# The turn between two layers: heads added early, a narrower last step, one more chunk kept

## The chip, the cores and the metric

The kernel runs on one core of one Trainium2 chip. The metric is device time in microseconds (us). A core has engines with a queue of instructions each: TensorE (PE; weight loads are shown as PEld), VectorE (DVE), ScalarE (ACT), GpSimd (POOL) and SyncE (SP), which here issues the loads. Loads go through one queue that is spread over 16 DMA engines. On-chip memory has 128 partitions; matrix products land in PSUM banks.

## The reference

Two tokens (B = 2) pass twice through the same pair of layers, in float32: attention over a cache, then a gated feed-forward block, each with a layer norm (no scale) and a residual.

```
B, D, H, Sk, Dh, F = 2, 448, 16, 4096, 256, 1792
attention:  q = (layernorm(x) @ wq) by head;  p = softmax(q . k_cache / 16)
            x = x + concat_over_heads(p @ v_cache) @ wo
block:      g = layernorm(x) @ W_gate;  g = g * (g > 0)
            x = x + (g * (layernorm(x) @ W_up)) @ W_down
order:      attention, block, attention, block (same caches and weights both times)
```

Keys and values of one head and token are 4 MB each. There are 32 such pairs, "units", so each attention reads 256 MB of cache, and the kernel has to read it twice except for what stays on chip.

## The kernel before

**The store.** On-chip memory holds an "arena" of 24 places of 1 MB ("units" in the code: 128 partitions by 2048 floats) and three single places of 896 KB (128 by 1792 floats). Keys and values of a unit come in four chunks of 1 MB (NC = 4), or as 2, 4 or 8 chunks in one load. A load of weights is 896 KB: seven for gate and up ("in"), four for down ("out", the last a half), one for the query and output weights of a head or pair of heads ("h", "q", "o").

**The order of loads.** A list (`pending`) is written by hand: all of the first attention, the first block's eleven weight loads, all of the second attention, the second block. `pump` (L159 issues on SP) walks down the list as long as the next load finds a place. `release` frees a place and calls `pump`, so a load is issued at the point of the program where a place becomes free, and on SP it waits until the engine that last read the place is done. The list is strict: a load that finds no place holds back all behind it.

**What stays on chip.** The second attention takes the units in the order: last four first. So the keys and values that the first attention reads last need not be loaded again. `keep` lists the chunks that stay: 20 chunks and the weights of the last head, and the last chunk (c = 3) of the values of `second[2]`. The other three chunks of those values (`rest`, c = 0, 1, 2) are let go at the turn, their places take 896 KB weight loads, and only the overwritten 896 KB of each is loaded again to the same place (`left_at`). With 21 chunks and a head kept, five places remain through the turn: the three of `rest` and two single ones.

**Attention.** For each unit: products of keys and query (VectorE, with ScalarE's sums), maximum and exponential (POOL, ACT), then `weigh` (L659): for each chunk four matmuls of 512 columns, side by side in four bands of PE's columns, that add p @ v into a bank `po`. For odd units the pair of units of a head is closed: `out_copy` (L673, ACT) copies the first 256 columns of the bank into `row`, `out_add` (L677, DVE) adds the other 256, `out_turn` (L688, PE) turns them into columns, `out_keep` (L701, DVE) divides by the sum of the exponentials, and `project` (L711, PE) multiplies by the output weights into the bank `acc`. `busy(n)` (L361) is a product of n times 64 columns that nobody reads; it only occupies PE.

**The turn.** After the last `project`, `ffn(False)` begins with `absorb` (L369 to L390): ACT copies `acc` to `row` and sums it (L379), PE turns `row` into columns and forms the mean (L381, L369, L371), and DVE adds both to x in its column form `xs` (L389). Then `proj` multiplies x by the gate and up weights (L809), four matmuls for each 896 KB of weights and each of its 128-row parts; the fourth load ("in", 3) holds the last 64 rows of both, and so is used twice, at the end of the gate half and at the start of the up half. Each part's place is released behind its last product. `add_rows` (L394) adds `acc` into the running x in row form (`y`) behind the gate half; `squares` and `deviation` (L405, L406) give the layer norm's scale. Then come the ReLU and product of both halves, the turning of the hidden values (L880), the down products (`block`, L903), and x for the second attention.

**Second attention, first units.** The keys kept are used first; each chunk released lets one of the next loads go, in the order of the program: four chunks of the first unit's keys, then keys of the second unit and values in turn.

Of the kernel before, what the change touches and what calls it, by code (L numbers as in the profile page):

```python
# [10 lines left out]
ALU = mybir.AluOpType  # L11
AX = mybir.AxisListType
# [14 lines left out]
KEPT = 20  # L27
ALONE = 25
SPARED = 12
TINY = 174  # L30
# [50 lines left out]
def two_layers(  # L81
# [55 lines left out]
    def pump(by_half=False):  # L137
        while pending:
            (kind, name, c), n = pending[0]
            last = at_of.get((kind, name, c - 1)) if kind in "kv" else None  # L140
            if kind == "g":
                last = MIDDLE - (name + 1) % 2
            at = units.take(n, kind, last)
            if at is None:
                return
            pending.pop(0)
            src = source((kind, name, c), n)
            assert at == left_at.get((kind, name, c), at)
            start = place(at) + VALUES * DH * (name in spared and n == PAIR)
            dst = arena[:, start : start + src.shape[1]]  # L150
            parts = [0, src.shape[1]]
            if by_half:
                parts[1:1] = [src.shape[1] // 2]
            if not pending:
                parts[1:1] = [src.shape[1] - CLOSE * TAIL]
            elif len(pending) == 1:
                parts[1:1] = [8 * P]
            for i, j in zip(parts, parts[1:]):
                nc.sync.dma_start(dst[:, i:j], src[:, i:j])  # L159
            for k in range(n):  # L160
                key = (kind, name, c + k)
                if n == PAIR:
                    key = ("k", name, k - NC) if k >= NC else ("v", behind[name], k)
                if kind == "g":
                    key = ("q", name, 0) if (name + k) % 2 == 0 else ("o", name - 1, 0)
                at_of[key] = at + k
                if kind == "in" and k:
                    lies_at[key] = start + k * F
            if n >= NC:
                blocks.add((kind, name))  # L170
# [85 lines left out]
    keep.add(("v", second[2], NC - 1))  # L256
    of_second = [(key, n) for key, n in of_second if key not in keep]

    rest = [("v", second[2], c) for c in range(NC - 1)]
    heads = [(key, n) for key, n in of_second if key[0] in "hq"][:2]  # L260
    parts = [(key, 1) for key in rest]
    first_of_second = parts[1:] + heads + parts[:1]
# [148 lines left out]
    def attention(order, after, q_first=None, begun=None):  # L411
# [228 lines left out]
        def weigh(u, c):  # L640


            vt = get("v", order[u], c)
            if (u - n_u, c) in FILL:
                busy(FILL[u - n_u, c])
# [5 lines left out]
            for t in range(CT // 2):  # L651
# [5 lines left out]
                for values, i, j in parts:  # L657
                    if i < j:
# [5 lines left out]
                            stop=(u % 2 == 1 and c == NC - 1),  # L664
                        )
            if ("v", order[u], c) not in after:
                release("v", order[u], c)
            if u >= n_u - 2 and c == NC - 1:
                busy(8)
# [33 lines left out]
        def project(u):  # L703
# [4 lines left out]
            for c in range(2):  # L708
# [4 lines left out]
                    start=(n < 3), stop=(n >= n_u - 3),  # L713
# [3 lines left out]
            if h < GROUPED:  # L717
                if h % 2:
                    release("o", h // 2, 0)
            elif ("h", h, 0) not in after:  # L720
                release("h", h, 0)

# [12 lines left out]
        for u in range(n_u + 2):  # L735

            mixed = ahead and u < HASTE
            if u == n_u - 1 and u not in q_of:
                query(u)
            if_pair(score, u, 0)  # L740
# [48 lines left out]
            if_pair(out_copy, u - 1)  # L789

    def ffn(last):
# [3 lines left out]
        busy(2)  # L795
        total = squares()
        if not last:
# [5 lines left out]
        def proj(p, parts):  # L803

            p = p[:, :D]
            for n, (part, c, done) in enumerate(parts):
                w = get("in", "", part)
# [12 lines left out]
            return p  # L820

# [28 lines left out]
        add_rows(SUMS, lead, stop=last)  # L850
# [164 lines left out]
    attention(first, keep)  # L1015
    attention(second, set(), *ffn(False))
# [67 lines left out]
```

## Time and profile before

| | us |
|---|---|
| median of 3 runs (1313.6 to 1314.62) | 1314.23 |
| profiled execution, its own time | 1314.3 |
| its span (first to last instruction) | 1312.0 |
| DVE busy | 1065.3 (81%) |
| PE busy | 505.6 (39%) |
| POOL busy | 297.9 (23%) |
| ACT busy | 195.2 (15%) |

The bytes read are 560.47 MB, at 427 GB/s over the span. The mean granted clock of TensorE is 0.69 of full speed. The engines' busy times overlap; a busy share says little of what bounds a stretch. The rows further down are copied from the page and from answers of the trace, which can be asked for a window of time, an engine or a line.

### The profile page before, as it was taken

Reading aid. Unit: us, or ns where it says so; the run is one execution under the profiler, and the core shown is the slowest. Engines: PE = TensorE matmul, PEld = TensorE weight load, DVE = VectorE, ACT = ScalarE, POOL = GpSimd, SP = SyncE. Lnnn points to the kernel's source line nnn. Section 1 sums busy time; section 2 is a strip of 40 time slices with the busy share of each in tenths; the row PEclk is TensorE's granted clock in tenths of the full one; section 3 lists DMA queues with packets and bytes.
Section 4 is the critical chain, followed back from the end, with each engine's and each line's share of the span. In section 5 each row is a group of like instructions: output and inputs, shape, how many; then the busy total and the mean of one; then the engine's idle time right before and its main releaser. Section 6 shows DMA issues by size and latency. Waiting matters only on the chain.

```text
span 1312.0 us, 8388 instructions
## 1 busy us (share of the span) xinstructions
PE 505.6 (39%) x3022; PEld 152.0 (12%) x3022; DVE 1065.3 (81%) x711; ACT 195.2 (15%) x789; POOL 297.9 (23%) x169
## 2 busy tenths in 40 slices
PE   3152243332433224324495445322342513433248
PEld 2010010000100001101141101100110100110013
DVE  4988988799897998787619896698999889886892
ACT  1100000010000000122417523000000100012231
POOL 0330412304123040021002151140345304100230
PEclk9665776657766577666697767666676666766669
DMA  9999999999999999999999999999999999999998
GB/s 408 438 432 432 434 426 438 438 426 434 434 430 432 438 432 424 443 420 429 422 399 421 434 427 439 438 436 430 423 443 432 430 430 438 432 432 427 429 421 337
DMA packets 20068, 561.00 MB, mean 428 GB/s; under 512 B 2232, under 2 KB 2364, under 8 KB 6844
## 3 DMA queue, kind: packets, MB, share of 16 engines
q1 hardware_dynamic: 20020, 560.48, 99.5%
q8 instruction: 23, 0.38, 0.1%
q14 instruction: 17, 0.14, 0.0%
q10 hardware_dynamic: 8, 0.00, 0.0%
HBM read 560.47 MB, written 0.00 MB: 427 GB/s over the span
## 4 chain that ended last, share of the span: by engine, by line
DMA 55%; DVE 31%; POOL 7%; PE 4%; issue 2%; ACT 1%; SPq 0%; POOLq 0%; DVEq 0%; ACTq 0%
DMA arena<-in_vk_dram 51%; DVE tiny L538 16%; DVE arena L524 10%; POOL tiny L629 4%; POOL tiny L601 4%; DMA arena<-in_w_in_dram 3%; DVE arena L573 2%; DVE arena L586 2%; DMA arena<-in_w_out_dram 1%; PE small L688 1%; PE po L453 1%; ACT arena L579 1%; DVE row L677 0%; DVE tiny L583 0%; ACT down L617 0%
## 5 line engine op out<-in xcount | busy, mean ns | idle before, releaser
L524 DVE TENSOR_TENSOR arena<-arena 128x8192 f32<-128x8192 f32 (+2 forms) x53 | 450.0, 8492 | 103.4 <-DMA arena<-in_vk_dram 102.6
L538 DVE TENSOR_REDUCE tiny<-arena 128x32 f32<-128x8192 f32 (+1 forms) x54 | 436.5, 8084 | 0.0
L659 PE MATMUL po<-arena,down 128*4 128x512 f32 x2052 | 313.2, 729 | 192.9 <-ACT down L617 116.5
L601 POOL PARTITION_ALL_REDUCE tiny<-tiny x63 | 121.0, 1920 | 719.2 <-DVE tiny L595 718.4
L688 PE MATMUL small<-tiny,row 128*128 128x2 f32 x128 | 30.9, 345 | 558.7 <-DVE row L677 558.7
L629 POOL PARTITION_ALL_REDUCE tiny<-tiny x63 | 149.0, 2364 | 60.4 <-ACT down L617 60.4
L613 ACT ACTIVATE tiny<-tiny 128x1 f32<-128x1 f32 x63 | 18.6, 295 | 734.6 <-POOL tiny L601 734.6
L659 PEld LDWEIGHTS po<-arena,down 128*4 128x4 f32 x2052 | 65.7, 97 | 410.5 <-issue 231.2
L688 PEld LDWEIGHTS small<-tiny,row 128*128 128x128 f32 x128 | 28.1, 306 | 589.1 <-DVE row L677 589.1
L453 PE MATMUL po<-arena,xs 128*33 128x512 f32 (+1 forms) x130 | 65.3, 661 | 0.0
L579 ACT ACTIVATE arena<-arena 128x256 f32<-128x256 f32 x135 | 54.4, 404 | 41.3 <-DVE arena L573 40.4
L711 PE MATMUL acc<-arena,tiny 128*2 128x448 f32 x128 | 51.0, 895 | 21.2 <-DVE tiny L701 21.1
L530 ACT ACTIVATE arena<-arena 128x256 f32<-128x256 f32 x112 | 44.8, 402 | 88.3 <-DVE arena L524 88.3
L465 POOL PARTITION_BROADCAST arena<-arena x32 | 21.8, 749 | 158.5 <-ACT arena L461 147.8
L573 DVE TENSOR_TENSOR arena<-arena 128x1024 f32<-128x1024 f32 (+2 forms) x21 | 32.8, 1560 | 3.4 <-PE acc L711 3.4
L677 DVE SCALAR_TENSOR_TENSOR row<-po,tiny,row 128x256 f32<-128x256 f32 x32 | 15.4, 480 | 22.1 <-ACT row L673 22.0
L461 ACT ACTIVATE arena<-po 33x512 f32<-33x512 f32 x13 | 7.7, 590 | 159.3 <-PE po L453 159.3
L701 DVE TENSOR_TENSOR tiny<-small,tiny 128x4 f32<-128x4 f32 x32 | 5.2, 161 | 28.6 <-PE small L688 28.6
L617 ACT ACTIVATE down<-tiny 128x32 f32<-128x32 f32 x64 | 26.6, 416 | 2.2
L579 ACT ACTIVATION_READ_ACCUMULATOR arena<-arena 128x1 f32 x135 | 25.2, 187 | 0.0
L453 PEld LDWEIGHTS po<-arena,xs 128*33 128x33 f32 x130 | 16.4, 136 | 62.1 <-issue 59.4
L530 ACT ACTIVATION_READ_ACCUMULATOR arena<-arena 128x1 f32 x112 | 21.0, 187 | 0.0
(174 smaller groups left out, 335.8 us busy)
## 6 DMA issues: line engine op xcount, KB each, us to landing
arena<-in_vk_dram SPq DMA_DIRECT2D x17, 4096.0 KB, 38.2
arena<-in_vk_dram SPq DMA_DIRECT2D x16, 2048.0 KB, 32.7
arena<-in_w_pair_dram SPq DMA_DIRECT2D x11, 1792.0 KB, 30.8
arena<-in_vk_dram SPq DMA_DIRECT2D x11, 1024.0 KB, 9.4
arena<-in_w_in_dram SPq DMA_DIRECT2D x12, 896.0 KB, 25.5
arena<-in_vk_dram SPq DMA_DIRECT2D x1, 6528.0 KB
arena<-in_w_head_dram SPq DMA_DIRECT2D x7, 896.0 KB, 22.0
arena<-in_w_out_dram SPq DMA_DIRECT2D x5, 896.0 KB, 19.6
```

The lines of the kernel that those rows point to most:

```text
L453: nc.tensor.matmul(q[:, cols], xs[:, c, :], w_c, start=(i == 0), stop=(i == len(parts) - 1))
L524: nc.vector.tensor_mul(part, part, q_of[u][:, None, :].to_broadcast([P, n, DH]))
L530: nc.scalar.activation(kt[:, t, :], kt[:, t, :], AF.Copy, accum_out=s_of[u][:, t : t + 1])
L538: nc.vector.reduce_sum(found, part, axis=AX.X)
L573: nc.vector.tensor_mul(part[:, :whole, :], kt[:, :whole, :], q_of[u][:, None, :].to_broadcast([P, whole, DH]),)
L579: nc.scalar.activation(part[:, t, :], part[:, t, :], AF.Copy, accum_out=found[:, t : t + 1])
L601: nc.gpsimd.partition_all_reduce(mx_of[u], mx, P, RED.max)
L617: nc.scalar.activation(found, s_of.pop(u).rearrange("p (k r) -> p k r", r=2), AF.Exp, bias=nm, scale=sr[:, b : b + 1], accum_out=rs,)
L629: nc.gpsimd.partition_all_reduce(total[:, b : b + 1], rs, P, RED.add)
L659: nc.tensor.matmul(po_of[u][32 * t : 32 * t + 4, (i - 2 * t) * DH : (j - 2 * t) * DH], p_of[u][:, at : at + 4], values[:, i * DH : j * DH] ...
L688: nc.tensor.matmul(pT_of[u][:, c, :], row[:, c * P : (c + 1) * P], pick[:, b : b + B], start=True, stop=True,)
L711: nc.tensor.matmul(acc[at : at + B], oT_of[h][:, c, :], wo[:, c * D : (c + 1) * D], start=(n < 3), stop=(n >= n_u - 3),)
```

## The change

- `LEFT = 2`: chunks 2 and 3 of the values of `second[2]` stay on chip (22 kept chunks instead of 21), and only chunks 0 and 1 are loaded again. Four places remain through the turn. The order of the first loads of the second layer becomes: weights of a head, two value chunks, weights of a head.
- The last value chunk of the first attention is loaded in two halves. `weigh` works on the first half as before (two matmuls of 512 columns), then the bank is closed and `out_copy` and `out_add` run; the second half goes as four matmuls of 256 columns, one for each 256 values, into another bank.
- `settle=early`: behind the last exponential, before the last unit's values, `early` adds all heads but the last to x (`absorb`, `add_rows`) and computes minus the mean over D of the last head's output weights (`means`).
- `last_out` replaces turning and dividing of the last pair: for each 128 columns a sum on DVE, a turning matmul and a multiplication. There is no `project` of this head into `acc`.
- In `ffn(False)`, `arrive` adds the last head to x part by part, with the output weights as the stationary operand and the head's two columns as the moving one (`give`), and the mean by `means`; part 0 ahead of the first gate product, part 1 and the tails behind it. The running `y` gets the last head by two matmuls behind the gate half, in place of one `add_rows`. `squares` moves behind the gate half.
- The place of head 14's weights is freed without a `pump`; the next `pump` finds it. Fillers of the last two units are cut (8 columns' worth of 64 to 4, two of 8 and one of 5 and 2 go, one of 1 comes).

```diff
+LEFT = 2
-TINY = 174
+TINY = 176
@@ pump
-            if by_half:
+            if by_half or (kind, name, c) == ("v", first[-1], NC - 1):
@@ two_layers
-    keep.add(("v", second[2], NC - 1))
+    keep |= {("v", second[2], c) for c in range(LEFT, NC)}
-    rest = [("v", second[2], c) for c in range(NC - 1)]
+    rest = [("v", second[2], c) for c in range(LEFT)]
-    first_of_second = parts[1:] + heads + parts[:1]
+    first_of_second = heads[:1] + parts + heads[1:]
@@ weigh
+            split = settle and (u, c) == (n_u - 1, NC - 1)
+            closes = bool(settle) and (u, c) == (n_u - 1, NC - 2)
             if (u - n_u, c) in FILL:
-                busy(FILL[u - n_u, c])
+                busy(4 if split else FILL[u - n_u, c])
-            for t in range(CT // 2):
+            for t in range(CT // 4 if split else CT // 2):
...
-                            stop=(u % 2 == 1 and c == NC - 1),
+                            stop=(u % 2 == 1 and c == NC - 1) or (closes and t >= CT // 4),
+            if split:
+                out_copy(u)
+                out_add(u)
+                po_of[u] = po[0]
+                for t in range(CT // 2):
+                    at = 2 * (c * CT + CT // 2 + t) - t % 2
+                    nc.tensor.matmul(
+                        po_of[u][32 * t : 32 * t + 4, :DH],
+                        p_of[u][:, at : at + 4],
+                        vt[:, (CT // 2 + t) * DH : (CT // 2 + t + 1) * DH],
+                        start=True, stop=True,
+                    )
+                return
-            if u >= n_u - 2 and c == NC - 1:
+            if u >= n_u - 2 and c == NC - 1 and not settle:
                 busy(8)
@@ project
+            elif settle and u == n_u - 3:
+                units.free.add(at_of.pop(("h", h, 0)))
+        def last_out():
+            u = n_u - 1
+            h, b = order[u - 1]
+            pT, oT = small(2, B), little("oT", 2, B)
+            for c in range(2):
+                at = slice(c * P, (c + 1) * P)
+                nc.vector.scalar_tensor_tensor(
+                    row[:, at], po_of[u][:, at], fold[:, 0:1], row[:, at],
+                    op0=ALU.mult, op1=ALU.add,
+                )
+                nc.tensor.matmul(pT[:, c, :], row[:, at], pick[:, b : b + B], start=True, stop=True)
+                nc.vector.tensor_mul(oT[:, c, :], pT[:, c, :], r_of[u - 1])
+            busy(1)
+            return oT
@@ attention, loop over u
+            if settle and u == n_u + 1:
+                return last_out()
+            if settle and u == n_u:
+                settle()
+    def early():
+        absorb(acc[:SUMS], SUMS, lead, nlead)
+        add_rows(SUMS, lead)
+        gives = output_weights(H - 1).rearrange("p (c d) -> p c d", c=2)
+        nc.vector.reduce_sum(means, gives, axis=AX.X)
+        nc.vector.tensor_scalar_mul(means, means, -1.0 / D)
@@ ffn
+            wo = output_weights(H - 1)
+            pt = small(DC, B)
+            minus, less = po[0][:, :B], little("less", B)
@@ proj
+                if not last and part < FULL and c == part:
+                    arrive(part)
+        def arrive(part):
+            if part == 0:
+                for c in range(2):
+                    nc.tensor.matmul(
+                        minus, means[:, c : c + 1].to_broadcast([P, P]), oT[:, c, :],
+                        start=(c == 0), stop=(c == 1),
+                    )
+                    give(0, slice(0, P), 0, c)
+                for c in range(2):
+                    give(1, slice(0, P), P, c)
+                nc.vector.tensor_copy(less, minus)
+                add(*spans[0], less[:, None, :].to_broadcast([P, DC, B]))
+                for i in range(2):
+                    add(slice(0, P), slice(i, i + 1), pt)
...
+        def give(i, p, at, c):
+            w = wo[:, c * D + at : c * D + at + p.stop - p.start]
+            nc.tensor.matmul(pt[p, i, :], w, oT[:, c, :], start=(c == 0), stop=(c == 1))
@@ ffn, behind the gate half
-        add_rows(SUMS, lead, stop=last)
+        if last:
+            add_rows(SUMS, lead, stop=True)
+        else:
+            total = squares()
+            for c in range(2):
+                nc.tensor.matmul(y, oT[:, c, :], wo[:, c * D : (c + 1) * D], start=False, stop=False)
@@ end
-    attention(first, keep)
-    attention(second, set(), *ffn(False))
+    means = little("means", 2, bufs=1)
+    oT = attention(first, keep, settle=early)
+    attention(second, set(), *ffn(False, oT))
```

## Rows read from the trace of the kernel before

**Rows 1.** The page: DMA busy share in 40 slices; the queue's packets, MB, share
```profile
DMA  9999999999999999999999999999999999999998
...
q1 hardware_dynamic: 20020, 560.48, 99.5%
```

**Rows 2.** Busy time by window: length, engines' busy us, PEclk, DMA share, GB/s
```profile
672.00:680.00 8.00, 7.19 (x51) 2.81 (x49) 1.50 (x6) 0.69 (x2) 0.00 (x0) 1.00 1.02 423
```

**Rows 3.** The same view by single microseconds (PE, PEld, DVE, ACT, POOL)
```profile
643.00:644.00 1.00, 0.65 (x4) 0.56 (x4) 1.00 (x3) 0.04 (x1) 0.00 (x0) 0.77 1.04 442
...
668.00:669.00 1.00, 0.95 (x10) 0.29 (x12) 0.89 (x6) 0.00 (x0) 0.00 (x0) 1.00 0.73 301
669.00:670.00 1.00, 1.00 (x16) 0.39 (x12) 0.05 (x1) 0.00 (x0) 0.00 (x0) 1.00 0.47 194
670.00:671.00 1.00, 1.00 (x16) 0.19 (x8) 0.00 (x0) 0.00 (x0) 0.00 (x0) 1.00 0.93 208
671.00:672.00 1.00, 1.00 (x10) 0.17 (x2) 0.00 (x0) 0.00 (x0) 0.00 (x0) 1.00 0.81 323
...
677.00:678.00 1.00, 0.57 (x8) 0.16 (x8) 0.00 (x0) 0.00 (x0) 0.00 (x0) 1.00 1.05 437
```

**Rows 4.** The chain that ended last, in order of time: start us, us, what
```profile
661.94 1.09 PE po L659 x8
...
664.10 0.61 PE small L688 x4
...
666.01 0.64 ACT row L379 x2
...
667.08 0.67 PE small L369 x6
...
668.01 0.27 DVE xs L389
...
668.32 1.75 PE po L809 x16
...
680.40 1.09 PE po L903 x28
...
796.93 32.08 DMA arena<-in_vk_dram
```

**Rows 5.** Timelines of ScalarE and of VectorE near 663: start, us, instruction, idle before
```profile
663.05 0.47 ACT L673 ACTIVATE row<-po,tiny 128x256 f32<-128x256 f32 x1 [9.26 <-PE po L659]
...
663.56 0.48 DVE L677 SCALAR_TENSOR_TENSOR row<-po,tiny,row 128x256 f32<-128x256 f32 x1 [9.09 <-ACT row L673]
```

**Rows 6.** Timeline of the load queue SP: start and length of issues
```profile
669.34 1.08 SPq L159 DMA_DIRECT2D arena<-in_w_in_dram  x2
...
673.71 2.63 SPq L159 DMA_DIRECT2D arena<-in_w_out_dram  x3
...
693.60 0.33 SPq L159 DMA_DIRECT2D arena<-in_vk_dram  x1
...
704.36 0.33 SPq L159 DMA_DIRECT2D arena<-in_vk_dram  x1
```

**Rows 7.** Issues at 0.72, 669.34, 670.09, 693.60, 704.36: KB, us to landing
```profile
arena<-in_w_head_dram SPq DMA_DIRECT2D x1, 896.0 KB, 4.8
...
arena<-in_w_in_dram SPq DMA_DIRECT2D x1, 896.0 KB, 5.6
...
arena<-in_w_in_dram SPq DMA_DIRECT2D x1, 896.0 KB, 7.3
...
arena<-in_vk_dram SPq DMA_DIRECT2D x1, 1024.0 KB, 7.4
...
arena<-in_vk_dram SPq DMA_DIRECT2D x1, 1024.0 KB, 7.3
```

**Rows 8.** Timeline of TensorE around the turn
```profile
655.34 1.02 PE L361 MATMUL po<-ident 128*2 128x512 f32 x2
...
671.53 0.92 PE L394 MATMUL acc<-row,tiny 96*2 96x448 f32 x2
```

More of the change, by code (lines that the diff above doesn't have):

```diff
@@ L409, in inverse, with attention @@
         nc.vector.reciprocal(rstd, rstd)
-    def attention(order, after, q_first=None, begun=None):
+    def attention(order, after, q_first=None, begun=None, settle=None):
         nsr = little("nsr", B, bufs=1)
@@ L712, in project @@
                     acc[at : at + B], oT_of[h][:, c, :], wo[:, c * D : (c + 1) * D],
-                    start=(n < 3), stop=(n >= n_u - 3),
+                    start=(n < 3), stop=(n >= n_u - (5 if settle else 3)),
                 )
@@ L788, in attention, with ffn @@
                     if_pair(weigh, u - 1, c)
-            if_pair(out_copy, u - 1)
-    def ffn(last):
+            if not (settle and u == n_u):
+                if_pair(out_copy, u - 1)
+    def early():
         absorb(acc[:SUMS], SUMS, lead, nlead)
-        busy(2)
-        total = squares()
-        if not last:
+        add_rows(SUMS, lead)
+        gives = output_weights(H - 1).rearrange("p (c d) -> p c d", c=2)
+        nc.vector.reduce_sum(means, gives, axis=AX.X)
+        nc.vector.tensor_scalar_mul(means, means, -1.0 / D)
+    def ffn(last, oT=None):
+        if last:
+            absorb(acc[:SUMS], SUMS, lead, nlead)
+            busy(2)
+            total = squares()
[3 more added lines that the diff above has]
+            minus, less = po[0][:, :B], little("less", B)
             h, b = second[0]
@@ L820, in proj, with add @@
             return p
+        def arrive(part):
[12 more added lines that the diff above has]
+                    add(slice(0, P), slice(i, i + 1), pt)
+            elif part == 1:
+                for c in range(2):
+                    give(2, slice(0, P), 2 * P, c)
+                for p, c in spans[1:]:
+                    add(p, c, less[:, None, :].to_broadcast([P, DC, B]))
+                add(slice(0, P), slice(2, FULL), pt)
+            else:
+                for c in range(2):
+                    for p, i in spans[1:]:
+                        give(i.start, p, FULL * P, c)
+                for p, c in spans[1:]:
+                    add(p, c, pt)
+                nc.vector.tensor_copy(xs[:, :, 32:], xs[:, :, 31:32])
+        def give(i, p, at, c):
+            w = wo[:, c * D + at : c * D + at + p.stop - p.start]
+            nc.tensor.matmul(pt[p, i, :], w, oT[:, c, :], start=(c == 0), stop=(c == 1))
+        def add(p, c, part):
+            x_c = xr[p, c]
+            nc.vector.tensor_add(x_c, x_c, part[p, c, :, None].to_broadcast(x_c.shape))
         def between(part):
@@ L849, in ffn @@
         pg = proj(banks[0], [(0, 0, True), (1, 1, True), (2, 2, True), (3, 3, False)])
-        add_rows(SUMS, lead, stop=last)
+        if last:
+            add_rows(SUMS, lead, stop=True)
+        else:
+            total = squares()
+            for c in range(2):
+                nc.tensor.matmul(y, oT[:, c, :], wo[:, c * D : (c + 1) * D], start=False, stop=False)
         if last:
```

## The prediction

> **What bounds the kernel now.** I read the slices of the span first, then the queues, then the chain of waits across the turn between the layers. The DMA digit is 9 in all but the last slice, and one queue holds 99.5% of sixteen engines' span for 560.48 MB [rows 1]: the kernel is a stream of loads, and a change in the time has to be bytes that are not loaded or a stretch in which the stream runs dry. Full, it moves 423 GB/s with the 896 KB loads of the turn [rows 2]. One stretch is not full: from 668 to 672 us the rates are 301, 194, 208 and 323 GB/s [rows 3], 1026 KB where 4 us at 423 would be 1692. So 666 KB, or 1.57 us of a mean engine's time, is lost at the turn.
>
> Why it is dry there: five 896 KB loads of feed-forward weights are issued ahead; the sixth waits until the first gate product has released its place. The chain shows the way to it: the last values' products from 661.94, their copy 663.05, the sum of both halves 663.56, the turning products 664.10, then x is brought up from 666.01, 667.08 and 668.01 to the gate product at 668.32 [rows 4, 5]. The next two loads are issued from 669.34 [rows 6].
>
> Does the loss reach the end? The load issued at 669.34 landed 5.6 us later (674.9); the next, issued 0.75 us behind it, after 7.3 us (677.4) [rows 6, 7]. The first load of the program, onto an empty queue, took 4.8 us; its bytes are 2.17 of that at 423 GB/s, so about 2.6 us is issue and landing. Then 669.34 + 2.6 + 2.17 = 674.1 would have been possible, and 674.9 was measured: for the engine that finishes last the queue was not empty, it had 0.8 us to spare. The dry stretch was idle time of engines that had run ahead. A load has landed when its last engine has, so I count the 1.57 us as mostly no loss, and a small delay there as mostly no cost.
>
> **The change part by part.** *Bytes.* Of the three value chunks that the first layer lets go and the second loads again, one more stays: 917,504 bytes less, 917,504 / 423 GB/s = 2.17 us [rows 2]. The last value chunk comes as two loads with rows half as long; I take a few per cent of its 1 MB (2.48 us at 423 GB/s), 0.1 us, between nothing and the 2.6 us of a load onto an empty queue, and near nothing because the queue is full there. Net -2.1 us. The stream is the bound, so nothing hides this.
>
> By the Trainium skill (DMA: Bandwidth & Descriptors, Anatomy of one DMA) a DMA of the GpSimd path takes about 2.0 us plus its bytes; if that held for each load in this queue, the extra load would cost 2.0 us and the sum would be -0.2. The two loads above landed 2.5 us apart, not 4.2, so here the fixed part lies under the queue.
>
> *One place less.* Four instead of five loads can be issued ahead, so the fifth must be issued 2.17 us earlier than the sixth was, at 667.2, for the queue to stand as before. The shorter turn has to pay for that, and I work out its length.
>
> TensorE before the last values: the last-but-one unit's products end at 655.34, where a 512-column filler starts [rows 8]. Now comes the early sum into x: from the end of the copy (666.01 + 0.64) to 668.0 it takes 1.3 us, and the running sum behind it 0.85 of the 0.92 in its row [rows 4, 8]. Its input, ScalarE's copy of the projections, is ready: that engine is idle for 9.26 us before 663.05 [rows 5]. A 512-column product group occupies 0.86 of the 1.0 in its row, a 256-column one half of that. So: filler 0.43, two value chunks 1.72, filler 0.43, third chunk 0.86, filler 0.43, first half of the last 0.86 (two products side by side last as long as four, since the filler alone shows 1.02). 1.3 + 0.85 + 4.73 = 6.9: 662.2. The half has landed by then. The second half lands where the whole did, about 661.9, and waits 0.3; its narrow products (between 0.5 and 1.0, half the columns with the whole tail) take 0.6, until 662.8.
>
> After that: copy and sum of the first half (0.47 and 0.48, [rows 5]) run beside the narrow products, until 663.3. Then, twice: a 128-column sum (between 0.27 and 0.48, I take 0.35, nearer the row of 96 columns), one turning product (between 0.31 and 0.61, I take 0.38) and a small multiplication (under 0.27, I take 0.2): 0.95 with gaps, 665.2. Then the mean and the first weights as stationary operand, two products at 0.67/3 and a tail, 0.6: 665.8. A copy and two sums into x, 0.6 (0.4 to 0.8, by the 0.27 row): 666.4. From gate product to issue it took 669.34 - 668.32 = 1.02: the issue comes at about 667.45 (666.5 to 668.5), 1.9 us earlier than now and 0.3 later than the 667.2 that would leave all as it is. The last engine has 0.8 us to spare: cost 0, at the late end 0.5. Engines that run ahead idle 0.3 us longer.
>
> *The projection of the last head into y* moves behind the gate products, as two matmuls in place of one: +0.85 us on TensorE. Behind it in line is the first product of the up half, which releases the fourth weights, before at 673.71 [rows 6] and now near 674.55; that now lets the first down weights in. Landings 2.17 us apart put the fourth weights at 674.9 - 4.34 = 670.6 and these at 679.3; 674.55 + 2.6 + 2.17 = 679.3. Nothing is left to spare and nothing is late: 0, up to 0.4. The first load behind the down weights is released by the first down product at 680.40 + 1.09 = 681.5 [rows 4]; due with the stream (679.3 + 2 x 2.17 + 1.1 for the half load + 2.17 = 686.9) it may be issued until 682.1: 0.6 to spare.
>
> *Second layer.* Its start hangs on the last gate/up weights and stays. Its first loads are issued as compute releases places, at the same times as now, while the stream is 2.1 us ahead. Two have the least room [rows 6, 7]: 1 MB issued at 693.60 landed after 7.4 us and one at 704.36 after 7.3; less 2.48 for the bytes and 2.6, that is 2.3 and 2.2 us. Less 2.1, 0.1 to 0.2 remains: cost 0 to 0.5, I take 0.2. Later there is ample room: 8 MB issued at 796.93 took 32 us to land [rows 4], of which 19.8 are bytes.
>
> *Other edits.* The early additions (six of up to 0.27) and the mean over 896 columns (at most 3.5 times the 0.48 of 256) fall on VectorE while it is idle for 9.09 us before 663.56 [rows 5]; without that cover they would cost up to 3.3 us. The fillers that go give nothing back. The order of head and value loads changes; both are wanted after the first units of the second layer.
>
> *Sum.* -2.17 + 0.1 + 0 (turn) + 0 (y) + 0.2 = -1.9 us. The profiled execution took 1314.3 (span 1312.0) against a median of 1314.23, so the two stand alike: 1314.23 - 1.9 = 1312.3.
>
> **Rivals.** *Given back at the next narrow place (17%).* The loads issued at 693.60 and 704.36 come too late for the last engine as well; their times are fixed by compute, so what the turn gains above some 1 us ends there. For it: the spare of 2.2 us equals the gain. Against it: it needs more than the 2.6 us that I take for issue and landing, and that was read off a cold start. Time: -1.0, 1313.2.
>
> *The dry stretch counts and shrinks (17%).* If the engine that ends the kernel is one of those that idled from 668 to 672, and the fifth load is issued before 666.5, some 1.0 of the 1.57 us is gained as well: -3.2, 1311.0. For it: nothing says which engine is last 640 us later. Against it: my sum gives 667.45.
>
> *The stream of four places stalls at half clock (8%): slower.* Place: TensorE between 663 and 675, where fillers go and short products with waits come. The granted clock fell within 643 to 644 us (0.77), with TensorE busy for 0.65 of it; it held 1.00 in 677 to 678 at 0.57 [rows 3]. By the Trainium skill (TensorE: Matmul & The Clock Gate, What's actually happening) the array is throttled unless activity releases it; these two rows alone don't settle it. At 1.2 GHz the work behind the fourth weights (0.85 + 1.7 + 0.85 = 3.4 us) takes 6.8: the first down weights are issued 3.4 us late, the down products and the start of the second layer follow. Price 3.4 to 6: +1.5 to +4, I take +3: 1317.2. It decides once TensorE is at 1.2 GHz for most of 668 to 675; one short drop delays the first issue by 0.9 and is mostly absorbed.
>
> *It brings nothing (6%).* The extra load keeps its fixed cost in the queue, or the four places run dry in turn: -0.2, 1314.0.
>
> **How the numbers follow.** The forecast, -1.5 to -2.5, has 52%. 0.2% is 2.6 us, about what a measurement of this kernel can tell from no change: the forecast and the first and last rivals (75%) lie within it, less 7% for the forecast's upper edge: 68%. Faster than 1311.6: the second rival and that edge, 24%. Slower than 1316.9: 8%. The likeliest case's own range is 1311.7 to 1312.9; to hold 8 in 10 it reaches to 1310.8 (the second rival) and 1314.2 (the give-back and no change).
>
> **What would show it.** Queue bytes 560.48 - 0.92 = 559.56 MB. The fifth gate/up load issued at 667 to 668, the gate product from about 666.4. A dry stretch of about the same depth, some 2 us earlier. The second layer's first loads landing 2 us earlier than now, with less than 0.5 us to spare. Granted clock 1.00 from 654 to 690. The prediction is wrong if the fifth load is issued after 669, if a second dry stretch appears near 675 or 704 to 708, or if the end moves by other than the bytes.

## The result, and the profile after

The changed kernel took 1316.49 us in the median (1314.92 to 1317.98, 14 runs) against 1313.97 for the kernel before (1313.46 to 1314.62, 14 runs): a ratio of 1.0021, interval 1.0014 to 1.0028. It is slower by 2.5 us (1.8 to 3.7), where 1.9 less was forecast. The profiled execution took 1315.26 us, span 1313.5: it is 1.2 us quicker than the median, so its trace can't show all of the loss.

The page has the bytes that were predicted, and the answer to [rows 1] shows nothing else:

```profile
DMA  9999999999999999999999999999999999999998
...
q1 hardware_dynamic: 20020, 559.56, 99.4%
```

0.92 MB less, and the queue is as busy as before. The windows at the turn (columns as in [rows 2, 3]; the last two are DMA busy share and GB/s, the one before them the granted clock) show where the time went:

```profile
667.00:668.00 1.00, 1.00 (x10) 0.36 (x2) 0.10 (x1) 0.00 (x0) 0.00 (x0) 0.82 0.42 172
668.00:669.00 1.00, 1.00 (x8) 0.77 (x11) 0.19 (x1) 0.00 (x0) 0.00 (x0) 0.50 0.82 172
669.00:670.00 1.00, 1.00 (x8) 0.00 (x0) 0.00 (x0) 0.00 (x0) 0.00 (x0) 0.50 0.57 179
...
676.00:677.00 1.00, 1.00 (x13) 0.43 (x17) 0.49 (x3) 0.70 (x2) 0.00 (x0) 1.00 0.57 229
677.00:678.00 1.00, 1.00 (x10) 0.30 (x2) 0.17 (x1) 0.00 (x0) 0.00 (x0) 1.00 0.12 43
678.00:679.00 1.00, 1.00 (x10) 0.16 (x8) 0.00 (x0) 0.00 (x0) 0.00 (x0) 1.00 0.94 165
...
686.00:687.00 1.00, 1.00 (x24) 0.78 (x26) 0.19 (x1) 0.15 (x2) 0.00 (x0) 1.00 1.19 280
```

Three things are to be seen. The stream now runs dry three times, not once. The clock falls from 2.4 to 1.2 GHz at the gate products, within 667 to 668 us. And in 668 to 669 the engines are busy for 0.82 of the time and move 172 GB/s, where 423 GB/s stood beside a share of 1.02 in [rows 2]: a busy DMA engine is not one at its rate.

The chain of waits (start, us, what), against [rows 4]:

```profile
662.04 0.48 ACT row L689
...
666.75 0.96 PE po L864 x8
667.71 0.94 PE small L909 x4
...
670.83 3.14 PE po L864 x16
673.97 1.82 PE acc L948 x4
...
682.82 1.09 PE po L1001 x28
...
690.96 0.42 DVE row L494
```

L864 are the gate and up products (L809 before), L948 the projection into y, L1001 the down products (L903 before), and L494 the copy of the query with which the second layer begins (L493 before). The turn itself is as short as predicted. The down products start 2.42 us later (682.82 against 680.40), although their bytes were to come no later. The load queue (issues: start, length, count) shows the steps between, against [rows 6]:

```profile
667.77 5.10 SPq L160 DMA_DIRECT2D arena<-in_w_in_dram  x3
677.05 4.08 SPq L160 DMA_DIRECT2D arena<-in_w_out_dram  x4
683.92 0.33 SPq L160 DMA_DIRECT2D arena<-in_w_head_dram  x1
...
692.89 15.92 SPq L160 DMA_DIRECT2D arena<-in_vk_dram  x9
```

The load issued at 667.77 landed after (answer to [rows 7])

```profile
arena<-in_w_in_dram SPq DMA_DIRECT2D x1, 896.0 KB, 5.0
```

5.0 us, on the stream's schedule. The two behind it, issued at 670.36 and 672.54, took 4.6 and 6.0 us, so the last of them landed at 678.5. The first down weights were issued at 677.05 where 674.55 was predicted.

What ends this stretch is the second layer's start. VectorE's timeline in the kernel before (start, us):

```profile
688.53 0.42 DVE L493 COPY row<-po 128x256 f32<-128x256 f32 x1 [0.66 <-PE po L959]
688.99 0.42 DVE L586 SCALAR_TENSOR_TENSOR arena<-arena,po 128x256 f32<-128x256 f32 x1
```

From here VectorE works without a gap through the kept units, and each unit it is through with frees the place of the next load: the first such load is issued 1.94 us after the copy in both kernels (690.47 before, 692.89 after, the copy at 688.53 and 690.96). The chain of the kernel before shows why this start can matter, and the prediction did not use it. From the copy on the chain is compute, most of it VectorE's:

```profile
688.99 7.96 DVE arena L586 x46
...
742.59 1.13 DVE arena L573
...
796.50 0.43 ACT arena L461
```

No load stands in it until the one that [rows 4] shows at 796.93. In the change the same chain reaches that load at 798.53, 1.60 us later, from a start 2.43 us later; the span is 1.5 us longer in this execution, and the median 2.5. The runs had to tell whether the start is the cause, and why 2.17 us of bytes show nowhere.

### The profile page after: what moved, and what is told of

Its sections match the earlier page's. It is cut to its first block, busy times and chain, and to the rows that moved or that the text cites. A ratio compares the mean times of both kernels' runs of the same rounds, so it can differ in the third digit from the quotient of the medians.

```text
span 1313.5 us, 8441 instructions
## 1 busy us (share of the span) xinstructions
PE 511.6 (39%) x3042; PEld 156.8 (12%) x3042; DVE 1068.7 (81%) x726; ACT 195.0 (15%) x789; POOL 303.7 (23%) x169
## 3 DMA queue, kind: packets, MB, share of 16 engines
q1 hardware_dynamic: 20020, 559.56, 99.4%
## 4 chain that ended last, share of the span: by engine, by line
DMA 52%; DVE 31%; POOL 7%; PE 7%; issue 2%; ACT 1%; SPq 0%; POOLq 0%; DVEq 0%; ACTq 0%
DMA arena<-in_vk_dram 49%; DVE tiny L539 15%; DVE arena L525 10%; POOL tiny L630 5%; POOL tiny L602 2%; DMA arena<-in_w_in_dram 2%; DVE arena L574 2%; PE po L662 2%; DVE arena L587 2%; DMA arena<-in_w_out_dram 1%; PE small L704 1%; PE po L864 1%; ACT arena L580 1%; DVE row L693 1%; DVE tiny L584 0%
## 5 line engine op out<-in xcount | busy, mean ns | idle before, releaser
L602 POOL PARTITION_ALL_REDUCE tiny<-tiny x63 | 95.0, 1508 | 712.9 <-DVE tiny L596 712.1
L630 POOL PARTITION_ALL_REDUCE tiny<-tiny x63 | 180.6, 2867 | 60.3 <-ACT down L618 60.3
```

The lines of the kernel that those rows point to most:

```text
L602: nc.gpsimd.partition_all_reduce(mx_of[u], mx, P, RED.max)
L630: nc.gpsimd.partition_all_reduce(total[:, b : b + 1], rs, P, RED.add)
```

## The experiments

Fourteen more kernels ran. The kernel before, run beside them, took 1313.79 to 1313.95 in the median. "Start" below is the copy that begins the second layer, read from VectorE's timeline of each profiled execution, and "traced" is the time of that same execution; "places" are loads that can be ahead at the turn.

| run | MB | places | start | traced us | median us | ratio, interval |
|---|---|---|---|---|---|---|
| before | 560.48 | 5 | 688.53 | 1314.3 | 1313.9 | |
| the change | 559.56 | 4 | 690.96 | 1315.26 | 1316.49 | 1.0021 (1.0014 to 1.0028) |
| e10 before, a load left out at the turn | 559.56 | 5 | 688.74 | 1314.03 | 1314.53 | 1.0003 (0.9994 to 1.0012) |
| e14 before, as much left out later | 559.56 | 5 | 688.46 | 1311.69 | 1311.65 | 0.9982 (0.9973 to 0.9991) |
| e16 before, start delayed | 560.48 | 5 | 690.76 | 1316.65 | 1316.65 | 1.0018 (1.0009 to 1.0027) |
| e9 one place more | 561.4 | 6 | 688.25 | 1316.3 | 1315.82 | 1.0016 (1.0007 to 1.0024) |
| e15 e9, start delayed | 561.4 | 6 | 690.04 | 1316.16 | 1316.46 | 1.0019 (1.0010 to 1.0028) |
| e8 before, gate 0.86 later | 560.48 | 5 | 689.14 | 1313.81 | 1313.81 | 1.0000 (0.9991 to 1.0009) |
| e13 before, gate 2.15 later | 560.48 | 5 | 692.18 | 1316.8 | 1314.93 | 1.0010 (1.0001 to 1.0019) |
| e1 change, fillers | 559.56 | 4 | 691.99 | 1316.48 | 1315.51 | 1.0014 (1.0005 to 1.0022) |
| e6 e1, y later | 559.56 | 4 | 690.78 | 1316.56 | 1315.93 | 1.0017 (1.0008 to 1.0027) |
| e2 change, five places | 560.48 | 5 | 690.59 | 1315.12 | 1315.71 | 1.0015 (1.0006 to 1.0024) |
| e7 e2, fillers | 560.48 | 5 | 690.80 | 1315.38 | 1313.99 | 1.0001 (0.9992 to 1.0010) |
| e12 e7, a load left out | 559.56 | 5 | 688.41 | 1313.14 | 1314.18 | 1.0001 (0.9992 to 1.0010) |
| e4 before, no fillers | 560.48 | 5 | 691.29 | 1316.08 | 1316.24 | 1.0021 (1.0012 to 1.0029) |
| e3 before, four places | 559.56 | 4 | 692.64 | 1317.76 | 1316.62 | 1.0022 (1.0013 to 1.0031) |

An interval is about 1.2 us to either side, so differences of a few tenths say nothing. A traced execution need not stand for the median: e7's was the slowest of its runs and its clock had fallen, and e13's took 1.9 us over the median. So a start is best read beside the traced time of its row. Among the rows with 560.48 or 559.56 MB, e14 aside, starts of 688.4 to 689.1 go with 1313.1 to 1314.3 us, and starts of 690.6 to 692.6 with 1315.1 to 1317.8, whichever of the two byte counts it is.

The texts put on record before each run name theories and ranges. The medians of e1, e3, e8, e9 and e14 fell into a stated range; e4, e6, e12, e13 and e15 missed the nearest by up to 0.25 us, e16 by 0.35, e7 by 0.4, e2 by 0.5 and e10 by 0.7.

**Clock or depth of the queue?** These came first: the theories were that the lower clock is the whole loss, or that four places are.

e1_fill: idle products in the new functions, so that the clock holds.

```
 last_out:  + busy(4); busy(2)   ahead of the loop;  + busy(3) in it;  busy(1) -> busy(4)
 arrive(0): + busy(3)            behind the products
```


> The changed kernel with idle products put back where TensorE waits for the last head (two before its first turning product, one behind it, one behind both, one before the first gate product; 16 times 64 columns in all). Theory A (the granted clock falls to 1.2 GHz at 667.6 and TensorE then lags the loads): the clock stays at 1.00 from 654 to 690, the first down weights are issued near 675 instead of 677.05, no second dry stretch at 676 to 679, 1312 to 1313.2 us, spread of the runs about 1 us. Theory B (four places are one too few at any clock): the second dry stretch stays, 1315.5 to 1317.

e2_five: the change with 21 kept units and five places.

```
-LEFT = 2
+LEFT = 3
-    first_of_second = heads[:1] + parts + heads[1:]
+    first_of_second = parts[1:] + heads + parts[:1]
-            elif settle and u == n_u - 3:
-                units.free.add(at_of.pop(("h", h, 0)))
```


> The changed kernel with 21 kept chunks as before, so five places through the turn and 0.92 MB loaded again; all else as changed. Theory A (clock): the clock still falls near 667.6, but one more load in the queue covers most of it: 1313.5 to 1315.2 us, spread still over 2 us. Theory B (places): with the shorter turn and five places no dry stretch is left and the kernel is faster than before: 1312.3 to 1313.3 us.

e3_four_before: the kernel before, turn untouched, with 22 units kept and the change's order of loads.

```
-    keep.add(("v", second[2], NC - 1))
+    keep |= {("v", second[2], c) for c in range(2, NC)}
...                                     (the order of loads, and head 14's place freed without a pump)
```


> The kernel before with 22 kept chunks (four places, 0.92 MB less) and its own long turn with all fillers. Theory A (clock): the clock stays up; the fifth load is issued at 669.3, 2.2 us late against before, of which 0.8 was to spare: bytes -2.2, dry +1.4: 1313.0 to 1314.0 us. Theory B (places): a second dry stretch near 675 to 679 as in the changed kernel, 1315.5 to 1317 us.

e4_before_unfilled: the kernel before without its idle products at the turn.

```
-            if u >= n_u - 2 and c == NC - 1:
+            if u >= n_u - 2 and c == NC - 1 and not after:
                 busy(8)
...                                     (likewise busy(2), busy(5) and the one ahead of squares; one of 8 cut to 4)
```


> The kernel before without the idle products of the turn (one of 8 cut to 4, two of 8, one of 5 and two of 2 left out, in the first attention and first block alone). Theory A (clock): the clock falls between 664 and 672 for at least 3.4 us and gate products last twice as long; five places cover part: 1314.4 to 1316 us, spread over 1.5 us. Theory B (places): within 0.3 us of before.

Each theory had its part and neither all. In e1 the clock held until 679 and 1.0 us came back in the median, which is within the noise; in e4 the clock fell at 666.74 and that alone cost 2.4 with the old turn and five places. Yet e3, whose clock was 1.00 until 678, lost 2.8. The windows of e1 show the queue short of work at full clock:

```profile
668.00:669.00 1.00, 1.00 (x12) 0.25 (x11) 0.19 (x1) 0.00 (x0) 0.00 (x0) 1.00 0.78 186
...
685.00:686.00 1.00, 0.95 (x16) 0.74 (x20) 0.19 (x1) 0.33 (x2) 0.00 (x0) 1.00 0.50 100
```

e7_five_fill adds e1's fillers to e2, and e6_fill_y moves the projection into y (L948) behind the first up product, so that the down weights are issued earlier.

```
-            for c in range(2):                                       (ahead of the up products)
-                nc.tensor.matmul(y, oT[:, c, :], ...)
+                if not last and (part, c) == (3, FULL + 1):          (behind the first of them)
+                    for k in range(2): nc.tensor.matmul(y, oT[:, k, :], ...)
```


> The changed kernel with five places (21 kept chunks) and the idle products of the first experiment. Theory A (clock): the clock stays up, the gate products start 1.5 us earlier than before the change and the queue has one load more than in the changed kernel: 1312.5 to 1313.6 us. Theory C (a queue that runs empty on all engines costs more than its idle time, as the engines start again together and their packets then take 0.5 to 1.9 us instead of 0.27): no engine's queue is empty, so also 1312.5 to 1313.6. Both fall if it stays above 1314.5.

> The changed kernel with the idle products of the first experiment and the last head's two matmuls into y moved behind the first product of the up half (the fourth place is released 1.7 us earlier). Theory A (TensorE lags the loads): 1312.3 to 1314 us. Theory C: the first dry stretch, at 666 to 671, stays and with it the slow packets: 1315 to 1315.8, as in the first experiment.

e7 missed its expectation and ended level with the kernel before. Its traced execution lost the clock within 666 to 667 all the same; e12, further down, has the same turn and fillers, held 1.00 until 696, and its start (688.41) is that of the kernel before. So with five places and the clock up, the new turn costs nothing and gains nothing. e6 is the clean case against the clock. It was granted 1.00 from 652 to 699, the first down weights were issued at 673.10, earlier than the 674.55 that the prediction wanted, and it was as slow as the change (0.6 us less, within the noise):

```profile
668.00:669.00 1.00, 1.00 (x12) 0.55 (x12) 0.19 (x1) 0.00 (x0) 0.00 (x0) 1.00 0.50 136
...
672.00:673.00 1.00, 1.00 (x11) 0.39 (x11) 0.45 (x3) 0.69 (x2) 0.00 (x0) 1.00 0.93 222
...
685.00:686.00 1.00, 1.00 (x22) 0.58 (x10) 0.00 (x0) 0.37 (x2) 0.00 (x0) 1.00 0.78 219
```

At 672 to 673 the loads at work had been issued in time, the engines count as busy for 0.93, and they move 222 GB/s. The chain of e6 shows what sets its start instead of the clock, against the same load, the last of the gate and up weights, in the kernel before:

```profile
670.65 8.95 DMA arena<-in_w_in_dram
```
```profile
670.09 7.29 DMA arena<-in_w_in_dram
```

It lands at 679.6 in e6 and at 677.4 before. In the change the chain runs through TensorE instead, at half clock until 674.47. With four places there are thus two limits that give nearly the same start (690.96 in the change, 690.78 in e6), and mending the clock alone bares the other.

One number sums up the turn: the MB that the queue moved up to 690 us, ahead of the first load that the second layer's start lets go (packets, MB, share; the kernel before, then the change):

```profile
q1 hardware_dynamic: 9371, 295.61, 99.7%
```
```profile
q1 hardware_dynamic: 9247, 293.91, 99.4%
```

The change is 1.70 MB behind, 4.0 us at 423 GB/s, of which 0.92 MB need not come at all. In the other traces, by places and granted clock in the gate products: five and 1.00, 295.79 (e12); five and 0.50, 294.93, 294.90 and 294.77 (e2, e7, e4); four and 1.00, 294.03, 293.89 and 293.81 (e1, e6, e3). Against the kernel before, the fallen clock costs 0.7 to 0.8 MB with five places and nothing more with four; the lost place costs 1.6 to 1.8 at either clock. These are single executions, but the groups do not overlap.

**Was the spare at the first load there?** e8_before_late and e13_before_later put idle products ahead of the gate products of the kernel before, 0.86 and 2.15 us of them; e9_six_before keeps 20 units and has six places, with the change's order of the first loads, so that the old dry stretch is covered.

```
         if not last:
+            busy(4)            (two of them in e8, five in e13)
```


> The kernel before with two idle products of 256 columns (0.86 us in all) ahead of the gate products of the first block: the sixth load is issued 0.86 us later, at full clock. My step of the prediction (the last engine has 0.8 us to spare) and theory A: 1313.8 to 1314.3 us. Theory C: the queue is then empty on all engines: more than the delay is lost, 1314.8 to 1316.

> The kernel before with five places and its clock, but 2.15 us of idle products (five calls, at the 0.43 us that each took in the run with two) ahead of the gate products: one late restart of the queue, everything behind it as deep as before. Theory A (a late restart costs its lateness beyond the spare of 0.8 us): 1.35 us more, 1315.0 to 1315.5. Theory B (a queue run dry for longer takes the price of a restart on top, as with four places): 1316.4 to 1318. Theory C (the idle time is made good later): 1313.8 to 1314.6.

> The kernel before with 20 kept chunks: six places, all four value chunks loaded again (0.92 MB more, +2.17 us), six loads issued ahead, no dry stretch. Theory A and the prediction's step (the dry stretch of before costs nothing): 1315.8 to 1316.3 us. Theory C: the dry stretch of before had a price and goes: 1313.8 to 1315.2.

e8 and e9 met the prediction's step to 0.2 us: a load 0.5 us later (669.87 for 669.34) costs nothing, and without the dry stretch of [rows 3] the kernel takes just its added bytes longer (2.0 of 2.17 us). e13's load was 1.79 us later (671.13), and its median came out at that lateness less the spare of 0.8 (1.0 measured, 1.35 expected for the full 2.15), though the stream stood nearly still:

```profile
671.00:672.00 1.00, 1.00 (x18) 0.28 (x12) 0.00 (x0) 0.00 (x0) 0.00 (x0) 1.00 0.17 59
```

So one late restart behind five places was priced rightly.

**What are the bytes worth?** e10_bytes leaves one load out at the turn of the kernel before, e12_five_fill_bytes the same in e7, and e14_deep_bytes as many bytes where the queue is deep.

```
+            if ((kind, name, c), n) == (rest[0], 1):                 (e10 and e12)
+                parts = []
+            if (kind, name, n) == ("k", second[14], PAIR) and len(pending) < len(of_second):
+                parts[-1] -= F                                       (e14)
             for i, j in zip(parts, parts[1:]):
                 nc.sync.dma_start(dst[:, i:j], src[:, i:j])
```


> The kernel before with its five places and its turn, but the last of the three chunks that come back behind the down weights is given its place and never loaded (the part of the attention over that chunk works on what lies there): 0.92 MB less on the queue, nothing else. Theory A (the step on the bytes was right, the place is what cost): 2.17 us less, 1311.5 to 1311.9. Theory B (in this stretch the bytes are no bound, other waits are): at most half of it, 1312.7 to 1313.8.

> The changed kernel with five places, fillers at the turn and 21 kept units, with the same load left out as in the run before it (the part of the attention over that chunk works on what lies there): the bytes of the change with its turn, and without its loss of a place. Theory A (the lost place is the whole loss): 2.17 us under the run with that load, 1311.6 to 1312.2. Theory B (the turn written anew costs something that the place hides): 1312.8 to 1314.

> The kernel before, with the same 0.92 MB left out as in the run that left a chunk out at the turn, but of a 4 MB load of the second layer's fifteenth unit, where loads land some 33 us after their issue (the attention of that unit works on what lies in that quarter of the place). Theory A (bytes count where many loads stand in the queue, and none at the turn, where compute sets the issues behind them): 2.17 us less, 1311.5 to 1312.0. Theory B (bytes are no bound in the second layer either): 1313.2 to 1314.2.

This is the pair that decides. The queue's line of e10 and of e14:

```profile
q1 hardware_dynamic: 19876, 559.56, 99.5%
```
```profile
q1 hardware_dynamic: 20020, 559.56, 99.5%
```

The same bytes, the same share. e14 takes them from a load of 8 MB (not 4, as its text has it), the one of 7296 KB here, which landed 40.2 us after its issue:

```profile
arena<-in_vk_dram SPq DMA_DIRECT2D x1, 7296.0 KB, 40.2
```

There they are worth 2.24 us (2.17 expected). Left out at the turn they are worth nothing: e10 is 0.6 us above the kernel before (-0.8 to 1.6), over the ranges of both its theories, and e12 is level with e7. The windows from 690 to 700 of the kernel before, and then of e10, show where they go:

```profile
690.00:700.00 10.00, 3.98 (x23) 2.53 (x21) 9.86 (x56) 8.50 (x37) 4.62 (x4) 0.91 1.02 418
```
```profile
692.00:693.00 1.00, 1.00 (x5) 0.50 (x6) 1.00 (x9) 0.69 (x5) 1.00 (x2) 1.00 0.81 248
...
698.00:699.00 1.00, 0.00 (x0) 0.00 (x0) 1.00 (x4) 0.41 (x2) 0.00 (x0) 0.99 0.97 238
690.00:700.00 10.00, 4.18 (x24) 2.70 (x22) 9.89 (x53) 8.50 (x37) 4.82 (x4) 0.95 0.97 347
```

VectorE is full in both (9.86 and 9.89 of 10 us), so the places come free at the same times: the loads behind are issued 0.20 us later in e10, each of them (690.67 for 690.47, 704.56 for 704.36). e10 has one load fewer in front of them, and its stream moves 347 GB/s where 418 went before: 0.71 MB less in 10 us, 1.7 us of the stream. Three loads of e10, issued at 693.80, 695.58 and 704.56, landed after

```profile
arena<-in_vk_dram SPq DMA_DIRECT2D x1, 1024.0 KB, 5.7
...
arena<-in_vk_dram SPq DMA_DIRECT2D x1, 1024.0 KB, 6.9
...
arena<-in_vk_dram SPq DMA_DIRECT2D x1, 1024.0 KB, 7.1
```

The first landed at 699.5, 1.5 us before its fellow of [rows 6, 7]; the last at 711.7, exactly with it. By then the 2.17 us are gone.

**Has the second layer's start any spare?** e16_before_delayed and e15_six_delayed put five idle products ahead of its query, in the kernel before and in e9.

```
+        for _ in range(5):
+            busy(4)
         nc.tensor.matmul(q, total.to_broadcast([P, P]), turn_cols, start=False, stop=False)
```


> The kernel before with the same 2.15 us of idle products ahead of the second layer's start. Theory A (its first issues have next to no spare behind five loads): 1.5 to 2.4 us more, 1315.4 to 1316.3. The prediction's step (2.2 us of spare at the loads issued at 693.60 and 704.36): 0 to 0.3 more, 1313.8 to 1314.3.

> The kernel before with 20 kept units and six places (one load more stands behind the down weights; 1315.82 by itself), and 2.15 us of idle products ahead of the last product of the query that the second layer starts with. Theory A (one load more is 2.17 us of cover for the second layer's first issues): the delay costs 0 to 0.5, 1315.8 to 1316.3. Theory B (a later start is a later end, whatever stands in the queue): 2.15 more, 1317.6 to 1318.2.

The copy on VectorE in e16, and in e15:

```profile
690.76 0.42 DVE L493 COPY row<-po 128x256 f32<-128x256 f32 x1 [2.91 <-PE po L959]
```
```profile
690.04 0.42 DVE L493 COPY row<-po 128x256 f32<-128x256 f32 x1 [2.91 <-PE po L961]
```

A start 2.23 us later, with not a byte changed, costs 2.8 us by the medians and 2.4 by the ratio (1.2 to 3.5): the spare of 2.2 us isn't there. With one load more in front, a start 1.79 us later than e9's costs 0.6. Together with e9 and e10 this fixes where the kernel before stands: at the corner of two bounds. One load more behind the down weights, and bytes decide (+2.0); one fewer, and the start decides (nothing gained). The change saves bytes on the side where they have no price, and moves the start, which has one.

## Why the prediction was wrong, step by step

Two terms of the sum failed: the second layer's spare (taken at 0.2 us) and the place given up (taken at 0). The first would have eaten the saved bytes had the turn kept its pace; the second is where its trace lost the stream.

**The second layer's spare.** "Less 2.1, 0.1 to 0.2 remains: cost 0 to 0.5, I take 0.2." With the bytes at -2.17, e10's +0.6 makes that term 2.75: all that the bytes were to bring was given back there. The prediction had the place and the reason ("their times are fixed by compute") and named the two loads; it gave the give-back 17% and half its size. Its 2.6 us for issue and landing was read off the one load that found sixteen idle engines. In e10 the load issued at 693.80 would have landed at 698.9 by it, and landed at 699.5; the next, issued at 695.58, landed 3.0 us behind it, where its bytes are 2.48, while the engines counted as busy for 0.97 of the stretch and moved 347 GB/s. One load more in front took the cost of a late start from 2.8 us to 0.6 (e16, e15): what decides in such a stretch is how many loads stand ahead, not the latency of one. The chain of the kernel before had a plainer sign: from the copy at 688.53 to 796.93 it waits for no load, so the start was on it, and the bytes that the change saves were not.

**One place less, "cost 0".** e1 against e12 (both with fillers, same bytes, four places against five): +1.3 us in the median, and 1.76 MB less on the queue by 690. In the change's own trace 1.70 of the 1.80 MB that the stream is behind by 742 (315.86 against 317.66) were lost by 690, ahead of the two loads of the second layer that the prediction watched. The first load was where I put it (667.77 for 667.45, landed in 5.0), and its spare was real (e8). But I followed one load where a queue of three or four is short at each release in turn: the second landed 2.2 us behind it, the third 1.4 us later than the stream would have brought it, and the down weights after them. "Its start hangs on the last gate/up weights and stays" had the right load, but that load came late: 678.5 in the change and 679.6 in e6, for 677.4 before. The prediction has this as half of a rival at 6% ("the four places run dry in turn"), priced at -0.2 us.

**The clock.** The rival at half clock had a chance of 8%; its place and mechanism are in the trace (0.50, which is 1.2 GHz, from 667.64 to 674.47; the projection into y 1.82 us for 1.50 in e12; the down weights 2.5 us later than forecast). With five places its price is clear: 2.4 us (e4 against the kernel before) and 1.7 (e2 against e7). With four it is 1.0 (the change against e1) or 0.6 (against e6), within the noise and under the 1.5 to 4 that the rival took; the chain of e6 shows the late weights behind it. Its rule, by the Trainium skill (TensorE: Matmul & The Clock Gate, What's actually happening), is that the throttle is the default and activity lifts it; the trace agrees that the clock fell among short products with waits between, and in e4 (0.50 from 666.74) it fell in the old turn too once the idle products were gone. Idle products do not hold it for sure: of the four traces of the new turn with fillers, three kept 1.00 through the gate products (e1, e6, e12) and one did not (e7). "The fillers that go give nothing back" asked only what their time costs.

**The sum.** -2.17 (bytes) + 2.75 (second layer) - 0.35 (new turn, e12 against e10, within its interval of nothing) + 1.33 (place) + 0.98 (clock) = +2.5. These are steps from one median to the next, so they meet the measured number by construction; each carries about 1.2 us of uncertainty, and since place and clock do not add up, another order of steps would share the loss out otherwise. Both end in a later start. e16 prices a start 2.23 us later at 2.4 to 2.8 us; the traced execution of the change, with its start 2.43 us later, took 1.0 us more than that of the kernel before.

**What was right.** The bytes in MB, and their price where the queue is deep: 2.24 us for a predicted 2.17 (e14). By the Trainium skill (DMA: Bandwidth & Descriptors, Anatomy of one DMA) a DMA has a fixed part besides its bytes; that it lies under the queue rests on the two loads of the prediction that landed 2.5 us apart, since e14 shortens a load and takes none away. e10 shows that the price of the bytes cannot be carried over to a shallow queue. The turn's length (gate product 666.75 for 666.4), the 0.8 us of spare at the first load (e8) and that the old dry stretch costs next to nothing (e9) held as well. "A second dry stretch near 675 or 704 to 708" was named as a sign of failure, and came at 676 to 679.

**What stays open.** Why loads that are issued in time, in a queue just restarted, move at half the rate: whether engines in step crowd one another, or work is fetched too late. No run separates these. Nor is it shown why starts that are nearly the same went with traced times 1.3 us apart (690.80 with 1315.38 in e7, 690.76 with 1316.65 in e16), or what the median of the change lost beyond its trace. No run beat the kernel before but e14, which leaves work out.

## What to carry to other kernels

Before you count a saved transfer at its bytes, look for the next load whose issue is set by compute, and count the loads that stand in front of it: only those beyond what covers it are worth their time. To find out cheaply, leave the same bytes out once there and once where the queue is deep. And give up a place of a queue, or the idle products that fill a wait, only after asking who is late when the queue runs dry at every release, not only at the first.

## What the hardware showed that I had not expected

- The busy share of the DMA engines is no measure of their rate in a shallow queue: 0.97 beside 347 GB/s over 10 us in e10, 1.02 beside 418 in the kernel before; 0.93 beside 222 in e6. The queue's share of the whole span was 99.4% in the slower kernel.
- Engines idled for 1.6 us on the mean in the kernel before without a loss that the medians show (e9), and 0.9 MB could be left out without a gain (e10).
- The repeated runs spread over 3 us in the change (1314.92 to 1317.98) and in e10 (1312.55 to 1315.49), and over 0.7 in e14 and e9.
- Four loads ahead in place of five left the queue 1.6 to 1.8 MB behind by 690 us at either clock.
